# Attention and a gated feed-forward layer on one core: five PSUM banks for the last blocks of a stage, two for its outputs, and the outputs two blocks later

## The chip, the cores and the metric

The kernel runs on one core of a Trainium2 chip. The metric is the device time of one execution in microseconds; lower is better. A core has several engines, each with its own instruction queue, which it works through in order: TensorE (PE in the profile; its weight loads are PEld) multiplies matrices and writes to PSUM; VectorE (DVE) and ScalarE (ACT) work element by element and read PSUM and SBUF; GpSimd (POOL) does hardly anything here; SyncE (SP) starts DMA transfers. They meet at semaphores. PSUM has eight banks; a bank holds 512 fp32 numbers for each of 128 partitions.

## The reference

```python
def phi(x):
    proj = np.einsum('bhsd,df->bhsf', x, w_phi)
    proj = proj - np.max(np.abs(proj), axis=-1, keepdims=True)
    return np.concatenate([np.exp(proj), np.exp(-proj)], axis=-1)
q_p, k_p = (phi(q), phi(k))
kv = np.einsum('bhsf,bhsd->bhfd', k_p, v)
z = np.sum(k_p, axis=2)
num = np.einsum('bhsf,bhfd->bhsd', q_p, kv)
den = np.einsum('bhsf,bhf->bhs', q_p, z)[..., None] + 1e-06
x = (num / den) ... reshaped to (tokens, model width)
gate = 1.0 / (1.0 + np.exp(-(x @ w_gate)))
val = x @ w_val
out = (gate * val @ w_out)
```

There are 8 batches, 8 heads, 576 positions and a head width of 64; so 4608 tokens with a model width of 512. The feed-forward layer is 1536 wide. The change touches only the feed-forward part.

## The kernel before, in words

The feed-forward width is cut into 12 pieces of 128 columns, called j. **Stage one** works out the attention and, between its steps, the feed-forward part of the first four j (`JA = 4`) for all tokens. **Stage two** (`rest_chunks`, L293) adds the other eight j. Every fp32 number is split into a high and a low part (xh and xl, wh and wl, hh and hl), and three matmuls (high by high, high by low, low by high) stand for one.

*The feed-forward work of stage one* is built by `half_units` (L200). Tokens come in 18 chunks of 256, numbered 0 to 17. A chunk has four **blocks**, one for each j; a block has two halves, the gate columns (m = 0) and the value columns (m = 1), of 12 matmuls each (`half`, L239, with `mm_in`, L157 to L165). The first half takes a PSUM tile gv of one bank for both. When both halves are issued, the generator `gate` (L219) is started. It issues tanh t and exp u on ScalarE (L226, L227), which read the gate half; three steps on VectorE (L230, L231, L232), of which L231 is the last to read the bank; then hh on ScalarE (L234) and hl on VectorE (L236). Tiles hh and hl have ten buffers. A chunk also has two **outputs**, one for each 128 of its tokens (`half_out`, L253): 12 matmuls, three for each j (`mm_out`, L167 to L173), into a PSUM tile acc, then a copy y to SBUF on ScalarE (L261) and a store on SP one step later (L265). An output needs hh and hl of all four blocks of its chunk.

A chunk's input is loaded by `load_x` (L203): a DMA on SP (L206), three steps of waiting, then xh on ScalarE (L209), and one step later xl on VectorE (L211). It is begun when block 0 of the chunk ahead has been issued, if the attention has stored all of the chunk.

*Order.* Stage one runs under a schedule written by hand: each engine gets its instructions in the order in which the Python code issues them. Generators such as `gate`, `load_x` and the attention's own steps wait in a list `tasks`; `tick()` (L195) advances each by one `yield`. Closures for halves and outputs stand in a list `ready`. The attention's loop (L756 to L784) calls `fill()` (L681) between its steps, which pops as many closures as a budget (`RATE`, with a cost of 1.45 for a half and 0.69 times four for an output) allows, with a `tick()` behind each. Chunks wait in `coming` until the attention has got far enough. What is left when the attention is through, all of chunks 15 to 17 and the rest of 13 and 14 that stands in `ready`, is issued by L785 to L790, one closure and one `tick()` after the other. `chunk` (L272) sets the order in a chunk: block 0, first output of the chunk ahead, block 1, second output of the chunk ahead, block 2, block 3. The last chunk's outputs follow at the end.

*PSUM in stage one* (L358 to L360): two banks for gv (pool `ps_gv`), five for everything that the attention multiplies (pool `ps_a`, tag a), one for acc (pool `ps_o`). In a pool with n buffers a new tile takes the bank of the tile n before it, and the first matmul into it waits until that tile's readers are through.

*Stage two* has TensorE's order written by hand; its other engines are ordered by a scheduler that plans with a simulated timeline and places their instructions among those of stage one where it sees room. Each weight tile comes as raw 64-bit words (L106) and is converted on VectorE by six steps (L80, L82, L87, L90, L93, L94), with one on ScalarE (L81) and a DMA (L85). The weights of j = 4 to 7 go to memory that the attention has left, and so are converted while chunks 15 to 17 are on TensorE; those of j = 8 to 11 go to memory that stage one's weights and tiles hold to its end. Stage two's input is split by L62 and L63 (in `split`, L61). Its PSUM tiles are g and v, two banks each, and four banks for acc.

Of the kernel before, what the change touches and what calls it, by code (L numbers as in the profile page):

```python
# [9 lines left out]
F32 = mybir.dt.float32  # L10
# [11 lines left out]
P = 128  # L22
NP = H // 2
DM = H * D
# [4 lines left out]
CH = 256  # L29
# [5 lines left out]
JA = 4  # L35
# [9 lines left out]
def attention_moe(  # L45
# [106 lines left out]
    def x_tiles(mp, w, name):  # L152
        xh = mp.tile([P, NC4 * w], F32R, tag="xh", name="xh" + name)
        xl = mp.tile([P, NC4 * w], F32R, tag="xl", name="xl" + name)
        return xh, xl, xl.bitcast(F32)

    def mm_in(o, xs, j, m, w):  # L157
        (xh, xl), (wh, wl) = xs, weights[j]
        i = 0
        for cc in range(NC4):  # L160
            ws = slice(m * DM + cc * P, m * DM + cc * P + P)
            cs = slice(cc * w, cc * w + w)
            for a, x in ((wh, xh), (wh, xl), (wl, xh)):
                nc.tensor.matmul(o, a[:, ws], x[:, cs], start=i == 0, stop=i == 11)  # L164
                i += 1  # L165

    def mm_out(acc, t, hs, j, first, last):  # L167
        (hh, hl, _), (wh, wl) = hs, weights[j]
        ts, ws = slice(t * P, t * P + P), slice(2 * DM, 3 * DM)
        for i, (a, w) in enumerate(((hh, wh), (hh, wl), (hl, wh))):  # L170
            nc.tensor.matmul(  # L171
                acc, a[:, ts], w[:, ws], start=first and i == 0, stop=last and i == 2
            )  # L173
# [16 lines left out]
    def start(g):  # L190

        if next(g, tasks) is not tasks:
            tasks.append(g)

    def tick():  # L195
        for g in list(tasks):
            if next(g, tasks) is tasks:
                tasks.remove(g)

    def half_units(js, mp, ps_gv, ps_acc, need):  # L200
        xs, hs, gvs, parts = {}, {}, {}, collections.Counter()

        def load_x(c):  # L203
            xh, xl, raw = x_tiles(mp, CH, f"1_{c}")
            xs[c] = xh, xl
            nc.sync.dma_start(raw, xscr[c])  # L206
            for _ in range(3):
                yield
            act.copy(xh, raw)  # L209
            yield  # L210
            vec.tensor_tensor(xl, raw, xh.bitcast(F32), op=ALU.subtract)  # L211
            parts[c] = NP

        def begin(c):
            free = c < 2 or parts["v", c - 2] == len(js)
            if c not in xs and free and parts["x", c] == CH * NP:
                start(load_x(c))

        def gate(c, i, n):  # L219
            gv = gvs.pop((c, i))  # L220
            u = mp.tile([P, CH], F32, tag="u", name="u" + n)
            t = mp.tile([P, CH], F32, tag="t", name="t" + n)
            hh = mp.tile([P, CH], F32R, tag="hh", name="hh" + n, bufs=10)
            hl = mp.tile([P, CH], F32R, tag="hl", name="hl" + n, bufs=10)
            hs[c, i] = hh, hl, None
            act.activation(t, gv[:, 0, :], AF.Tanh, scale=0.5)  # L226
            act.activation(u, gv[:, 0, :], AF.Exp)  # L227
            yield
            tu = t.bitcast(U32)
            vec.tensor_scalar(tu, tu, 0x7FFFFFFF, None, op0=ALU.bitwise_and)  # L230
            vec.scalar_tensor_tensor(t, t, 1.0, gv[:, 1, :], op0=ALU.add, op1=ALU.mult)  # L231
            vec.scalar_tensor_tensor(u, u, 1.0, t, op0=ALU.min, op1=ALU.mult)  # L232
            yield
            act.copy(hh, u)  # L234
            yield
            vec.tensor_tensor(hl, u, hh.bitcast(F32), op=ALU.subtract)  # L236
            parts["h", c] += 1

        def half(c, i, m):  # L239
            while parts[c] < NP:  # L240
                begin(c)
                tick()
            need(js[i], m)
            n = f"1_{c}_{js[i]}"
            if m == 0:
                gvs[c, i] = ps_gv.tile([P, 2, CH], F32, tag="gv", name="gv" + n)
            mm_in(gvs[c, i][:, m, :], xs[c], js[i], m, CH)
            if m == 1:
                parts["v", c] += 1
                start(gate(c, i, n))  # L250
                begin(c + 1)

        def half_out(c, t):  # L253
            need(js[-1], 2)
            while parts["h", c] < len(js):
                tick()
            acc = ps_acc.tile([P, DM], F32, tag="acc", name=f"acc1_{c}_{t}")
            for i, j in enumerate(js):
                mm_out(acc, t, hs[c, i], j, i == 0, i == len(js) - 1)
            y = mp.tile([P, DM], F32, tag="y", name=f"y1_{c}_{t}")  # L260
            act.activation(y, acc, AF.Copy, scale=0.5)  # L261

            def store():
                yield
                nc.sync.dma_start(yscr[c][t], y)  # L265

            start(store())

        def unit(c, i):
            return [(1.45, lambda m=m: half(c, i, m)) for m in range(2)]  # L270

        def chunk(c):  # L272

            items = []
            for i in range(len(js)):
                items += unit(c, i)
                if i < 2:
                    items += outs(c - 1)[i : i + 1]
            return items

        def first():

            items = []
            for i in range(len(js)):
                items += unit(0, i) + unit(1, i)
            return items + outs(0)

        def outs(c):
            return [(0.69 * len(js), lambda t=t: half_out(c, t)) for t in range(2)]

        return chunk, first, outs, begin, xs, parts
# [60 lines left out]
    with ExitStack() as actx:  # L352
        actx.enter_context(tc.manual_schedule())
        wp1 = actx.enter_context(tc.tile_pool(name="wp1", bufs=1))
        moe = actx.enter_context(tc.tile_pool(name="moe1", bufs=2))
        at1 = actx.enter_context(tc.tile_pool(name="at1", bufs=1, side="right"))
        at = actx.enter_context(tc.tile_pool(name="at", bufs=2, side="right"))
        ps_gv = actx.enter_context(tc.tile_pool(name="ps_gv", bufs=2, space=PSUM))  # L358
        ps_a = actx.enter_context(tc.tile_pool(name="ps_a", bufs=5, space=PSUM))
        ps_acc = actx.enter_context(tc.tile_pool(name="ps_o", bufs=1, space=PSUM))  # L360
# [290 lines left out]
                t += w  # L651

        weighed = []

        def need(j, m):

            while len(weighed) <= 3 * j + m:
                grant(3 * j + m + 1)
                tick()

        chunk, first, outs, begin, xs, parts = half_units(list(range(JA)), moe, ps_gv, ps_acc, need)
        ready, coming = [], []
        cdone = wdone = spot = after = 0
        wq = []
# [16 lines left out]
        def fill(n=TICKS):  # L681
            nonlocal due, spot, after
            spot += 1
            if coming and coming[0][0] <= spot + AHEAD and coming[0][1]:
                begin(coming[0][2][0])
            while coming and coming[0][0] <= spot:
                b, cs = coming.pop(0)[1:]
                after = spot + 4 * NP + (0 if b else 6 + LAG[1] - LAG[0])
                if b == 0:
                    ready.extend(first())  # L690
                else:
                    for c in cs:
                        ready.extend(chunk(c))
            left = (coming[0][0] if coming else after) - spot
            due += min(RATE, sum(c for c, _ in ready) / max(1, left))
            while ready and due >= ready[0][0] / 2:
                cost, f = ready.pop(0)
                f()
                tick()
                due -= cost  # L700
                n -= 1
            for _ in range(n):
                tick()
# [52 lines left out]
        for i in range(EARLY - 1, N + 1):  # L756
            if EARLY <= i:
                load(i + 2)
                grant(3 * (i - 1))
            if i + 1 < N:  # L760
                keys(i + 1)
                copies(q_half(i + 1, 0))
                fill()
                copies(q_half(i + 1, 1))
                rest(i + 1)
                start(q_max(i + 1))
                fill()
            if i < EARLY:
                fill()
                fill()  # L770
                continue
            if i < N:
                kv(i)
            if i > EARLY:
                num(i - 1)
                if i % NP == 0:
                    queue(i // NP - 1)
            fill()
            if i < N:
                turn(i)  # L780
                start(q_exp(i))
                if i + 2 < N:
                    load_v(i + 2)
            fill()  # L784
        for _, _, cs in coming:  # L785
            for c in cs:
                ready.extend(chunk(c))
        for _, f in ready + outs(NCHUNK - 1):
            f()
            tick()  # L790
# [75 lines left out]
```

## Time and profile before

| | |
|---|---|
| median of three runs | 1295.95 us (1295.61 to 1300.03) |
| the profiled execution | 1297.41 us |
| its span (first to last instruction) | 1295.6 us |
| granted TensorE clock, mean | 0.97 |
| busy: TensorE, weight loads | 1228.6 us (95%), 970.1 us (75%) |
| busy: VectorE, ScalarE | 797.9 us (62%), 526.8 us (41%) |

A row of the timeline begins with the start in microseconds from the span's start and the duration; then come engine, line, operation, the tile written and the tiles read. Brackets hold the idle time of the engine just before, and behind the arrow what ended it. In a list of waits, "PE gv L164 <- DVE t L231" says that a matmul of L164 into gv waited for the VectorE instruction of L231. Tile names leave out buffer numbers, so all blocks look alike; which block a row belongs to follows from TensorE's written order, with 24 matmuls a block and 12 an output.

### The profile page before, as it was taken

To read this page: it belongs to the slowest core of one execution; us is meant where nothing else is said; L and a number is where in the kernel's file an instruction comes from. 1 tells how busy PE (TensorE), PEld (TensorE's weight loads), DVE (VectorE), ACT (ScalarE), POOL (GpSimd) and SP (SyncE) were. 2 spreads that over 40 slices of the span, in tenths; PEclk is the share of its full clock that TensorE was granted. 3 is DMA by queue.
4 is the path that set the end of the run, shared out by engine and by line. 5 is a ranking of instruction groups with operands and counts; after the bars stand their busy time and mean duration, and the time that the engine had idled before them with its cause. 6 is when DMAs were issued, how large, how long until landed. Compare 5 with 4: busy or idle time off the path is not lost.

```text
span 1295.6 us, 22470 instructions
## 1 busy us (share of the span) xinstructions
PE 1228.6 (95%) x9120; PEld 970.1 (75%) x9120; DVE 797.9 (62%) x1608; ACT 526.8 (41%) x1081; POOL 0.7 (0%) x6
## 2 busy tenths in 40 slices
PE   7848899999999999999889999999999999999998
PEld 5535566777777777777778888888888888888886
DVE  6699888788878778883894953424343434333333
ACT  4535556665565566564443422222222222222221
POOL 0000000000000000000000000000000000000000
PEclk8967899999999999999899999999999999999999
DMA  4556344343343334332763620202011111111010
GB/s 175 178 178 243 105 124 136 98 137 97 124 127 111 110 104 126 105 109 72 264 209 133 209 98 1 83 15 71 28 58 40 57 42 46 52 39 60 5 61 33
DMA packets 80868, 131.55 MB, mean 102 GB/s; under 512 B 18300, under 2 KB 37884, under 8 KB 80764
## 3 DMA queue, kind: packets, MB, share of 16 engines
q1 hardware_dynamic: 80764, 130.11, 30.9%
q8 instruction: 72, 1.18, 0.4%
q14 instruction: 32, 0.26, 0.1%
HBM read 92.04 MB, written 28.45 MB: 93 GB/s over the span
## 4 chain that ended last, share of the span: by engine, by line
PE 81%; DVE 11%; ACT 3%; issue 2%; DMA 2%; SPq 0%; DVEq 0%; ACTq 0%
PE acc L171 21%; PE g L164 15%; PE v L164 15%; PE gv L164 12%; PE kvz L528 5%; PE nm L580 4%; PE pq L411 2%; PE dp L591 2%; PE pk L421 2%; ACT eq L564 1%; PE kvz L542 1%; DMA wraw<-w_moe 1%; PE pk L482 1%; DVE mb L513 1%; PE tp L554 1%
## 5 line engine op out<-in xcount | busy, mean ns | idle before, releaser
L164 PE MATMUL gv<-xh,wh 128*128 128x256 f32 x576 | 174.5, 303 | 17.0 <-ACT xh L62 11.9
L171 PE MATMUL acc<-wh,hh 128*128 128x512 f32 x432 | 172.4, 399 | 3.4 <-ACT hh L234 2.7
L164 PE MATMUL gv<-xl,wh 128*128 128x256 f32 x576 | 167.2, 290 | 2.8 <-DVE xl L211 2.8
L171 PE MATMUL acc<-wh,hl 128*128 128x512 f32 x432 | 169.2, 392 | 0.7 <-DVE hl L236 0.7
L171 PE MATMUL acc<-wl,hh 128*128 128x512 f32 x432 | 169.1, 392 | 0.0
L164 PE MATMUL gv<-xh,wl 128*128 128x256 f32 x576 | 166.5, 289 | 0.0
L164 PEld LDWEIGHTS gv<-xh,wh 128*128 128x128 f32 x576 | 114.1, 198 | 34.6 <-issue 14.9
L62 ACT CAST hh<-u 128x512 fp32r<-128x512 f32 x72 | 44.7, 621 | 229.4 <-DVE u L185 229.4
L183 DVE TENSOR_SCALAR t<-t 128x512 uint32<-128x512 uint32 x72 | 30.7, 426 | 167.2 <-ACT t L180 167.2
L164 PEld LDWEIGHTS gv<-xl,wh 128*128 128x128 f32 x576 | 114.1, 198 | 3.9 <-DVE xl L211 3.0
L180 ACT ACTIVATE t<-g 128x512 f32<-128x512 f32 x72 | 43.0, 598 | 179.5 <-PE g L164 179.3
L164 PEld LDWEIGHTS gv<-xh,wl 128*128 128x128 f32 x576 | 114.0, 198 | 0.0
L164 PE MATMUL g<-xh,wh 128*128 128x512 f32 x288 | 113.0, 392 | 0.0
L164 PE MATMUL v<-xh,wh 128*128 128x512 f32 x288 | 112.6, 391 | 0.0
L164 PE MATMUL g<-xh,wl 128*128 128x512 f32 x288 | 112.5, 391 | 0.0
L164 PE MATMUL g<-xl,wh 128*128 128x512 f32 x288 | 112.5, 391 | 0.0
L164 PE MATMUL v<-xl,wh 128*128 128x512 f32 x288 | 112.3, 390 | 0.0
L164 PE MATMUL v<-xh,wl 128*128 128x512 f32 x288 | 112.1, 389 | 0.0
L184 DVE SCALAR_TENSOR_TENSOR t<-t,v 128x512 f32<-128x512 f32 x72 | 49.4, 686 | 97.7 <-PE v L164 97.7
L171 PEld LDWEIGHTS acc<-wh,hh 128*128 128x128 f32 x432 | 81.1, 188 | 26.2 <-issue 4.8
L171 PEld LDWEIGHTS acc<-wh,hl 128*128 128x128 f32 x432 | 81.2, 188 | 20.2 <-DVE hl L236 1.7
L171 PEld LDWEIGHTS acc<-wl,hh 128*128 128x128 f32 x432 | 81.3, 188 | 15.8
(92 smaller groups left out, 2120.5 us busy)
## 6 DMA issues: line engine op xcount, KB each, us to landing
wraw<-w_moe SPq DMA_DIRECT2D x36, 512.0 KB, 4.6
xl<-xs SPq DMA_DIRECT2D x34, 512.0 KB, 3.9
k<-k SPq DMA_DIRECT2D x32, 320.0 KB, 3.7
v<-v SPq DMA_DIRECT2D x32, 320.0 KB, 2.9
q<-q SPq DMA_DIRECT2D x32, 288.0 KB, 4.1
wh<-wtop SPq DMA_DIRECT2D x36, 256.0 KB, 2.3
ys<-y SPq DMA_DIRECT2D x36, 256.0 KB, 2.0
yp<-ys SPq DMA_DIRECT2D x36, 256.0 KB
```

The costliest lines, as they stand in the source:

```text
L62: a = act.copy(h, x)
L164: nc.tensor.matmul(o, a[:, ws], x[:, cs], start=i == 0, stop=i == 11)
L171: nc.tensor.matmul(acc, a[:, ts], w[:, ws], start=first and i == 0, stop=last and i == 2)
L180: act.activation(t, g, AF.Tanh, scale=0.5)
L183: vec.tensor_scalar(tu, tu, 0x7FFFFFFF, None, op0=ALU.bitwise_and)
L184: vec.scalar_tensor_tensor(t, t, 1.0, vl, op0=ALU.add, op1=ALU.mult)
L411: nc.tensor.matmul(pps[hd], wk[head(hd), :], x[head(hd), cs], start=True, stop=True)
L421: nc.tensor.matmul(pps[hd][:, t, :], kx[head(hd), t * P : t * P + P], wk[head(hd), :], start=True, stop=True,)
L482: nc.tensor.matmul(pp[:, 0, :], kx[:, 4 * P :], wk, start=True, stop=True)
L528: nc.tensor.matmul(kvz[o : o + Q, : 2 * F], vx[:, 2 * t + hd, o % D : o % D + Q], (e0, e1)[hd][:, t, :] if t < 4 else e2[:, 0, :], start=t ...
L580: nc.tensor.matmul(nms[hf][o : o + Q, :], w[:, sg, o : o + Q], es[sg][:, o // D, cs], start=sg == 0, stop=sg == 1, tile_position=(0, o),)
L591: nc.tensor.matmul(dp[o : o + Q, :], w[:, 2, z : z + Q], es[sg][:, hd, hf * HS : hf * HS + HS], start=sg == 0, stop=sg == 1, tile_position ...
```

## The change

Two things change for the feed-forward closures that are issued behind the attention's loop. The pools from which gv and acc are taken become entries of a dictionary, which `half` and `half_out` look up when they run; behind the loop the entries are replaced: gv then comes from the attention's five banks, acc from the two that gv had. And for the chunks that still wait in `coming` there, `chunk(c, 2)` puts the outputs of the chunk ahead behind block 2 and block 3 instead of 0 and 1. Closures that stand in `ready` already keep their place.

```diff
-    def half_units(js, mp, ps_gv, ps_acc, need):
+    def half_units(js, mp, homes, need):
...
             if m == 0:
-                gvs[c, i] = ps_gv.tile([P, 2, CH], F32, tag="gv", name="gv" + n)
+                ps, tag = homes["gv"]
+                gvs[c, i] = ps.tile([P, 2, CH], F32, tag=tag, name="gv" + n)
...
-            acc = ps_acc.tile([P, DM], F32, tag="acc", name=f"acc1_{c}_{t}")
+            ps, tag = homes["acc"]
+            acc = ps.tile([P, DM], F32, tag=tag, name=f"acc1_{c}_{t}")
...
-        def chunk(c):
+        def chunk(c, at=0):
 
             items = []
             for i in range(len(js)):
                 items += unit(c, i)
-                if i < 2:
-                    items += outs(c - 1)[i : i + 1]
+                if 0 <= i - at < 2:
+                    items += outs(c - 1)[i - at : i - at + 1]
             return items
...
+        homes = {"gv": (ps_gv, "gv"), "acc": (ps_acc, "acc")}
...
-        chunk, first, outs, begin, xs, parts = half_units(list(range(JA)), moe, ps_gv, ps_acc, need)
+        chunk, first, outs, begin, xs, parts = half_units(list(range(JA)), moe, homes, need)
...
+
+        homes.update(gv=(ps_a, "a"), acc=(ps_gv, "gv"))
         for _, _, cs in coming:
             for c in cs:
-                ready.extend(chunk(c))
+                ready.extend(chunk(c, 2))
         for _, f in ready + outs(NCHUNK - 1):
             f()
             tick()
```

## The prediction

> **What bounds the kernel now.** I read the page first, then TensorE's waits, then the stretch in which the change acts, engine by engine.
>
> ```profile
> span 1295.6 us, 22470 instructions
> PE 81%; DVE 11%; ACT 3%; issue 2%; DMA 2%; SPq 0%; DVEq 0%; ACTq 0%
> ```
>
> TensorE carries 81% of the chain that ended last, so time is won where TensorE waits or runs at a low clock. The stretches below (window, PE, PEld, DVE, ACT and POOL busy, granted clock, DMA share, GB/s) surround the change. In block names, 15.2 is block 2 of chunk 15, and o15.0 is that chunk's first output (12 matmuls).
>
> ```profile
> 624.10:635.12 11.02, 5.28 (x27) 4.88 (x27) 10.46 (x23) 5.54 (x8) 0.00 (x0) 0.69 0.87 318
> 635.12:649.22 14.10, 14.10 (x98) 13.09 (x96) 14.10 (x30) 6.63 (x14) 0.00 (x0) 1.00 0.61 205
> 680.29:691.66 11.37, 11.37 (x85) 10.88 (x84) 4.46 (x12) 3.62 (x9) 0.00 (x0) 1.00 0.12 46
> 635.12:698.58 63.46, 57.19 (x363) 50.70 (x362) 49.65 (x114) 24.91 (x55) 0.00 (x0) 0.97 0.48 158
> 698.58:760.00 61.42, 61.42 (x270) 50.50 (x269) 48.88 (x94) 22.16 (x35) 0.00 (x0) 1.00 0.50 167
> ```
>
> Until 635.12 TensorE stands for chunk 15's input; block 15.0 comes before any moved output, so this stays. From 635.12 to 698.58 come eleven blocks (15.1 to 17.3) and eight outputs (o14.0 to o17.1): this is the stretch that changes. From 698.58, where the second stage begins, TensorE is busy throughout, so what the stretch loses in length the kernel should lose. VectorE is full at first (14.10 of 14.10: it also converts the second stage's weights) and mostly idle from 680 on (4.46 of 11.37).
>
> TensorE's waits from 635 to 698.7 are these four groups (total, times, longest), 6.3 us together:
>
> ```profile
> PE acc L171 <- ACT hh L234: 2.7, 3, 1.4
> PE gv L164 <- DVE t L231: 2.2, 2, 1.5
> PE acc L171 <- ACT y L261: 0.7, 1, 0.7
> PE acc L171 <- DVE hl L236: 0.7, 2, 0.4
> ```
>
> TensorE in order of time (start, duration, the idle time before it and its releaser in brackets):
>
> ```profile
> 599.96 1.41 PE L591 MATMUL dp<-eq,kv 128*32 128x288 f32 x16
> 627.21 0.38 PE L164 MATMUL gv<-xh,wh 128*128 128x256 f32 x1 [2.90 <-ACT xh L209]
> 635.12 0.40 PE L171 MATMUL acc<-wh,hh 128*128 128x512 f32 x1
> 640.72 0.40 PE L171 MATMUL acc<-wh,hh 128*128 128x512 f32 x1
> 643.47 0.28 PE L164 MATMUL gv<-xh,wh 128*128 128x256 f32 x1
> 649.10 0.28 PE L164 MATMUL gv<-xh,wl 128*128 128x256 f32 x1
> 650.85 0.39 PE L164 MATMUL gv<-xh,wh 128*128 128x256 f32 x1 [1.47 <-DVE t L231]
> 657.46 0.50 PE L171 MATMUL acc<-wh,hh 128*128 128x512 f32 x1 [1.42 <-ACT hh L234]
> 658.63 0.80 PE L171 MATMUL acc<-wh,hl 128*128 128x512 f32 x1 [0.44 <-DVE hl L236]
> 659.23 0.41 PE L164 MATMUL gv<-xh,wh 128*128 128x256 f32 x1
> 661.79 0.34 PE L164 MATMUL gv<-xh,wh 128*128 128x256 f32 x1
> 695.73 0.50 PE L171 MATMUL acc<-wh,hh 128*128 128x512 f32 x1 [0.69 <-ACT y L261]
> 698.58 0.39 PE L164 MATMUL g<-xh,wh 128*128 128x512 f32 x1
> ```
>
> Two undisturbed blocks hold 48 matmuls; the first to the last takes 649.10 - 643.47 = 5.63 us for 47 steps, so 0.12 us each and 2.87 a block. An undisturbed output takes 643.47 - 640.72 = 2.75. Eleven blocks and eight outputs are 31.6 + 22.0 = 53.6 us; the stretch takes 63.46. **9.9 us are lost here**, 0.76% of the span. The waits are 6.3 of it. The rest is mostly matmuls spaced wide after a wait: from 659.23 to 661.79 twelve steps take 2.56 us where 1.44 would do.
>
> A sentence on that from the Trainium skill, "TensorE: Matmul & The Clock Gate", section "HAM oscillation — how this bites in real kernels": the clock is lost to idle gaps above about 3.4 us. The waits ahead of 659.23 are far shorter and the spacing doubled all the same, so by the page those 1.1 us would not go with the waits, and the ceiling would be 8.8 instead of 9.9.
>
> **The change part by part.**
>
> *Five banks for the blocks.* Nothing is added: the same matmuls write, the same gate reads. A block now waits for the gate five blocks back, not two. The attention's last matmuls start at 599.96, and its last bank is copied out by 601.49 + 0.40 (row below), and the pool hands out its oldest bank first; so that costs nothing. It removes the t L231 waits, 2.2 us and what follows them.
>
> *Two banks for the outputs.* Removes the y L261 wait, 0.7 us. The bank that an output takes was read by a gate two or more blocks earlier, so no wait is added.
>
> *Outputs behind blocks 2 and 3.* An output needs the hl of the preceding chunk's block 3. Before, one block and nine of its own matmuls stood between them; now three blocks do. For the last chunk, o16.1 stands between 17.3 and o17.0. This removes the hh L234 and hl L236 waits, 3.4 us. Each moved step also issues a copy y on ScalarE and a store on SP. On ScalarE y now stands ahead of hh of blocks 2 and 3 instead of 0 and 1; it waits for TensorE only, which will be ahead, so 0. On SP the store passes weight loads; nobody needs it before the second stage. o16.1, o17.0 and o17.1 follow each other and y has two buffers:
>
> ```profile
> ys<-y SPq DMA_DIRECT2D x36, 256.0 KB, 2.0
> ```
>
> o17.1's copy comes 5.5 us after o16.1's, the store between lands in about 2.0: nothing. Eight of ten hh/hl buffers are live at most: nothing.
>
> *What is late next: the gates.* Blocks and outputs without waits would end, counted on from 635.12: 15.3 at 646.5, 16.1 at 655.0, o15.1 at 666.2, 16.3 at 663.5, 17.2 at 674.8, o16.0 at 677.6, 17.3 at 680.5, o16.1 at 683.2, o17.1 at 688.7. The gates run on ScalarE and VectorE in a written order: tanh t and u, three VectorE steps, hh, then the next gate's t. So they have a pace of their own (first the attention's last copy out of a bank, then t and hh of a gate beside a mostly idle VectorE; then the t of 15.1, 15.2, 15.3, 16.0, 16.1 and, further on, 16.3):
>
> ```profile
> 601.49 0.40 ACT L607 COPY dr<-dp 128x288 f32<-128x288 f32 x1 [0.83 <-PE dp L591]
> 604.48 0.38 ACT L226 ACTIVATE t<-gv 128x256 f32<-128x256 f32 x1 [2.59 <-PE gv L164]
> 606.24 0.41 ACT L234 CAST hh<-u 128x256 fp32r<-128x256 f32 x1 [1.10 <-DVE u L232]
> ...
> 641.65 0.37 ACT L226 ACTIVATE t<-gv 128x256 f32<-128x256 f32 x1
> 647.46 0.38 ACT L226 ACTIVATE t<-gv 128x256 f32<-128x256 f32 x1
> 652.08 0.38 ACT L226 ACTIVATE t<-gv 128x256 f32<-128x256 f32 x1
> 657.32 0.38 ACT L226 ACTIVATE t<-gv 128x256 f32<-128x256 f32 x1
> 663.48 0.38 ACT L226 ACTIVATE t<-gv 128x256 f32<-128x256 f32 x1 [1.10 <-PE gv L164]
> 673.89 0.38 ACT L226 ACTIVATE t<-gv 128x256 f32<-128x256 f32 x1
> ```
>
> Beside the conversions a gate that waits for no block takes 4.6 (647.46 to 652.08) to 5.2 us (652.08 to 657.32), middle 4.9, and 5.8 with a chunk's xl in it (641.65 to 647.46); without them 606.24 + 0.41 - 604.48 = 2.2. TensorE would ask for one in 17.0 / 4 = 4.25 us. So the gates fall behind while conversions last, until about 680. Their t: 15.1 at 641.7 as now, 15.2 at 647.5, 15.3 at 652.1, 16.0 at 657.3, 16.1 at 662.2, 16.2 at 668.0, 16.3 at 672.9, 17.0 at 677.8, then 680.0, 682.2, 684.4. VectorE's rows for what hangs on them (hl of the undisturbed gate; a conversion step; xl of chunk 17; u of 16.1; hl of 16.3):
>
> ```profile
> 606.67 0.42 DVE L236 TENSOR_TENSOR hl<-u,hh 128x256 fp32r<-128x256 f32 x1
> 658.70 0.69 DVE L90 SCALAR_TENSOR_TENSOR wraw<-wraw 128x512 uint32<-128x512 uint32 x1
> 663.11 1.23 DVE L211 TENSOR_TENSOR xl<-xl,xh 128x1024 fp32r<-128x1024 f32 x1
> 666.99 0.42 DVE L232 SCALAR_TENSOR_TENSOR u<-u,t 128x256 f32<-128x256 f32 x1
> 679.48 0.42 DVE L236 TENSOR_TENSOR hl<-u,hh 128x256 fp32r<-128x256 f32 x1
> ```
>
> - Banks: the tightest is 17.3, whose turn comes at 677.6 and needs 16.2's t L231, which precedes its u, 3.5 us behind its t (666.99 - 663.48), so done by 671.5. Covered by 6.
> - Outputs: o16.0's tenth matmul is due at 677.6 - 0.7 = 676.9 and needs hl of 16.3, now at 679.48 + 0.42 = 679.9, 6.0 behind its t at 673.89, and then at 672.9 + 6.0 = 678.9: late by 2.0. o17.0's is due at 685.3; hl of 17.3 ends at 684.4 + 606.67 + 0.42 - 604.48 = 687.0: late by 1.7.
> - Input: the loader counts scheduler steps, and with the output gone from between blocks 0 and 1 xl of chunk 17 moves on VectorE from ahead of 16.1's gate to behind its u. That u ends at 662.2 + (666.99 + 0.42 - 663.48) = 666.1; with a conversion step of 0.69 and its own 1.23 it ends near 668, and 17.0 wants it at 666.3: late by 1.7.
>
> These three are the same lateness: a wait at 17.0 shifts the later dues too. So about 2.0 us once, plus 0.5 for wide spacing behind it. The stretch would end at 688.7 + 2.5 = 691.2. **Gain 9.9 - 2.5 = 7.4 us.** Bounds: gates that keep up leave 9.9; gates at 5.8 throughout put 16.1's t at 664.9, 17.0's xl near 670.7, 4.4 late, with spacing about 5.4, leaving 4.5. I take the middle pace because it comes from the two rows in which no block was awaited.
>
> The second stage's weights for j from 8 on are converted behind the release of the old ones by the last output, so that work shifts along with TensorE; it ran beside a TensorE without idle time (61.42 of 61.42): 0.
>
> The profiled execution took 1297.41 us, 1.8 outside its span; less 7.4 it is 1290.0. The three runs' median, 1295.95, lies 1.5 lower. From it: **1288.6 us**. About 0.5%, 6.5 us, is what a measurement of this kernel tells from no change; the line is at 1289.5.
>
> **The rivals.**
>
> 1. *The waits come back as waits for gates.* The written ScalarE and VectorE orders, not banks, are the limit, and conversions fill them. For it: VectorE's 14.10 of 14.10. Against it: its idle time after 680, into which gates can drain. At the pace of 5.8 the gain is 4.5, 1291.5; if the weight work is also re-ordered unfavourably by a single step per gate (0.69, for seven gates, 4.8), it is nothing, 1296. The Trainium skill speaks for this side in the same page and section: adding PSUM double-buffering to its thin-M kernel gave no further gain. Here t L231 stands among the releasers, so the trace agrees only in part.
> 2. *The gates pile up and the tail pays, slower.* With five banks TensorE can be five blocks ahead at 17.3 (680.5); o17.0 must then wait for all five. At 4.9 each they take 24.5 us, less 4.8 covered by o16.1 and nine matmuls: 19.7 lost, 9.8 more than gained, 1305.8. It turns slower by over 0.5% when five gates take 21.2, above 4.2 each. That needs conversions among them after 680, but all VectorE work of the stretch is 49.65 us, which would be done by 684.8.
> 3. *It doesn't do what it says.* If most blocks left were handed out before the banks are switched, little changes: 1296. Block 15.0 starts at 627.21, 26 us behind the attention's last group at 599.96 + 1.41, so I give it almost nothing.
>
> **How the numbers follow.** Forecast (gain 6.5 to 9.9): 0.56. Rival 1: 0.34, all within 0.5%. Rival 2: 0.06. Rival 3: 0.04, no change. Faster 0.56, same 0.38, slower 0.06. The range runs from the full 9.9 and 0.6 of spread between runs, 1285.5, to a gain of 2, 1294.0, which leaves out rival 2, rival 3 and the worst of rival 1.
>
> **What the changed profile would show.** Right: no waits on t L231 and y L261; the sum of waits between the stretch's ends about 2 us, on xl L211, hh L234 or hl L236 around 17.0, o16.0 or o17.0; the second stage's first g near 691; granted clock 0.99 there. If the first g stands at 695 or later, with hh or xl as releasers, rival 1; if one long wait stands ahead of o17.0, rival 2. If TensorE waits after the first g, the statement on the weights is wrong; if block 15.0 starts elsewhere than at 627, the order ahead of it was re-drawn, which I held fixed.

## The result, and the profile after

The changed kernel took 1289.43 us (median of six, 1286.48 to 1292.08), the kernel before 1297.98 us in the six runs that go with it. The ratio is 0.9931, interval 0.9914 to 0.9948: about 0.7% faster, where 7.4 us or 0.57% had been forecast. The profiled execution took 1289.85 us. From the page after, the span and the chain that ended last, which still runs over TensorE:

```profile
span 1288.1 us, 22464 instructions
...
PE 81%; DVE 10%; ACT 3%; DMA 3%; issue 2%; SPq 0%; DVEq 0%; ACTq 0%
```

The stretches of the kernel after, with the columns as before (window and its length, busy time of PE, PEld, DVE, ACT, POOL, clock, DMA share, GB/s):

```profile
625.43:636.48 11.05, 5.36 (x28) 4.96 (x27) 10.49 (x23) 5.54 (x8) 0.00 (x0) 0.69 0.88 323
636.48:690.86 54.38, 53.65 (x361) 49.35 (x360) 49.03 (x114) 24.07 (x55) 0.00 (x0) 1.00 0.55 184
690.86:752.00 61.14, 61.14 (x269) 50.28 (x268) 48.33 (x93) 21.77 (x35) 0.00 (x0) 1.00 0.51 168
```

VectorE does the same work as before, 49.03 against 49.65 us, in a shorter time, and TensorE's clock is 1.00 instead of 0.97. The second stage has no idle time again. TensorE's waits from 598 to 760:

```profile
PE gv L164 <- ACT xh L209: 2.8, 1, 2.8
PE gv L164 <- DVE xl L211: 2.8, 1, 2.8
PE acc L171 <- ACT hh L234: 0.7, 1, 0.7
PE nm L582 <- ACT eq L566: 0.4, 1, 0.4
```

The first two are chunk 15's input, as before. Of the 6.3 us in the stretch one wait of 0.7 is left. TensorE in order of time:

```profile
628.56 0.39 PE L164 MATMUL gv<-xh,wh 128*128 128x256 f32 x1 [2.85 <-ACT xh L209]
636.47 0.28 PE L164 MATMUL gv<-xh,wh 128*128 128x256 f32 x1
667.72 0.28 PE L164 MATMUL gv<-xl,wh 128*128 128x256 f32 x1
678.30 0.39 PE L171 MATMUL acc<-wh,hh 128*128 128x512 f32 x1
687.54 0.50 PE L171 MATMUL acc<-wh,hh 128*128 128x512 f32 x1 [0.73 <-ACT hh L234]
691.09 0.39 PE L164 MATMUL g<-xh,wh 128*128 128x512 f32 x1
```

Block 15.1 begins at 636.47 and the first g at 691.09. Call the time from the matmul behind block 15.0 to the first g the **stretch**: 54.62 us after, 63.46 before, 53.6 without any wait. It gave 8.84 us. The span fell by 1295.6 - 1288.1 = 7.5 only, because this execution came to 15.0 at 628.56 and the one before at 627.21, 1.35 later. That was lost ahead of everything that the change touches: up to the first moved output the rows of TensorE, VectorE and ScalarE come in the same order in both kernels. What follows the first g is 597.0 us in both.

A stretch differs between executions too. The changed kernel once more had 56.36, the kernel before once more 63.74, so the gain is 7.1 to 9.1 us. The start of 15.0 differs as well: the changed kernel once more came to it at 626.59, the kernel before once more at 628.21.

### The profile page after: what moved, and what is told of

Its sections match the earlier page's. It is cut to its first block, busy times and chain, and to the rows that moved or that the text cites. A ratio compares the mean times of both kernels' runs of the same rounds, so it can differ in the third digit from the quotient of the medians.

```text
span 1288.1 us, 22464 instructions
## 1 busy us (share of the span) xinstructions
PE 1221.7 (95%) x9120; PEld 964.7 (75%) x9120; DVE 798.1 (62%) x1608; ACT 525.4 (41%) x1081; POOL 0.7 (0%) x6
## 4 chain that ended last, share of the span: by engine, by line
PE 81%; DVE 10%; ACT 3%; DMA 3%; issue 2%; SPq 0%; DVEq 0%; ACTq 0%
PE acc L171 21%; PE g L164 15%; PE v L164 15%; PE gv L164 11%; PE kvz L530 5%; PE nm L582 4%; PE pq L413 2%; PE dp L593 2%; PE pk L423 2%; ACT eq L566 1%; PE kvz L544 1%; DMA wraw<-w_moe 1%; PE pk L484 1%; DMA rb<-den 1%; DVE t L231 1%
```

## The experiments

All stretches, in us, beside 53.6 without waits. Two numbers in a row are two executions; every other row is one.

| banks | order of outputs | conversions | stretch |
|---|---|---|---|
| as before | as before | as before | 63.46, 63.74 |
| new | as before | as before | 61.95 |
| as before | new | as before | 62.49 |
| five for blocks, one for outputs | new | as before | 59.58 |
| new | new | as before | 54.62, 56.36 |
| new | new, chunk 17's input later | as before | 60.30 |
| as before | as before | half the VectorE work | 59.30 |
| new | new | half the VectorE work | 53.56 |
| as before | as before | behind the last gate | 55.57, counted as said below |
| as before | as before | split | 62.79 |
| new | new | j = 4 held back | 62.80 |
| new | new | split | 53.63 |

**Banks alone.**

```diff
-                ready.extend(chunk(c, 2))
+                ready.extend(chunk(c))
```

> The changed kernel with its banks, but with the outputs behind blocks 0 and 1 as before. The stretch is counted from the matmul behind block 15.0 to the second stage's first g: 63.5 us before, 54.6 with the whole change, 53.6 without any wait. Theory (the gates' pace on ScalarE and VectorE sets when hh of a chunk's block 3 is there, and the bank waits are only spent ahead of the same lateness): the waits on t L231 vanish, those on hh L234 at o15.0 and o16.0 grow by as much; only the wait on y L261 is truly saved. Stretch 62 to 62.6, gain about 1 us. Rival (each wait is a loss by itself): the t L231 waits go with what follows them, stretch 59.8, gain 3.7 us.

Measured: 1296.32 us, ratio 0.999 (0.9978 to 1.0003), stretch 61.95. All waits in the stretch:

```profile
PE acc L171 <- ACT hh L234: 4.9, 3, 4.0
PE acc L171 <- DVE hl L236: 0.7, 2, 0.4
```

The waits on t L231 and y L261 are gone, and hh L234 grew from 2.7 to 4.9: at o15.0 it is 4.0 where it was 1.4. The bank wait had only been spent ahead of the same late gate. The theory holds.

**Order alone.**

```diff
-        homes.update(gv=(ps_a, "a"), acc=(ps_gv, "gv"))
```

> The changed kernel with its order of outputs, but with two banks for blocks and one for outputs as before. Theory (gates have a pace of about 4.7 us while VectorE converts): no wait on hh or hl at o15.0 and o16.0, but with two banks TensorE is held to the gates' pace at the three blocks that now follow each other without an output between: several waits on t L231, together 3 to 5 us; the y L261 wait stays. Stretch 58 to 59.5, gain 4 to 5.5 us. Banks and order together gave 8.8, so the sum of the two alone is less than both. Rival (each wait is a loss by itself): t L231 stays at 2.2 us in two waits, stretch 57.2, and both gains alone add up to the whole.

Measured: 1298.73 us, ratio 1.0002 (0.999 to 1.0015), stretch 62.49. The profiled execution came to 15.0 some 7 us late, so only its stretch is compared. In it:

```profile
PE gv L164 <- DVE t L231: 5.4, 4, 1.7
...
PE acc L171 <- ACT y L263: 1.6, 3, 0.7
```

The kind of wait is the one expected, its size was not: the stretch is 3 us longer than the range. The waits of 5.4 and 1.6 us, and 1.9 that goes with them (62.49 - 53.6 - 7.0), eat all but 1 us of the gain. It was not the clock, which stood at 1.00 in this stretch:

```profile
642.33:704.82 62.49, 55.47 (x363) 49.73 (x361) 49.30 (x114) 24.15 (x55) 0.00 (x0) 1.00 0.49 161
```

The banks alone give 1.5 and the order alone 1.0; both give 7.1 to 9.1. They are not two savings but one: each lets TensorE run ahead of late gates only if the other does too.

**One bank for the outputs.**

```diff
-        homes.update(gv=(ps_a, "a"), acc=(ps_gv, "gv"))
+        homes.update(gv=(ps_a, "a"))
```

> The changed kernel with five banks for blocks and the new order, but one bank for the outputs. Theory: only the three outputs that follow each other at the end (o16.1, o17.0, o17.1) and those behind gates that are late pay: y L261 waits of 0.7 at o17.0 and o17.1 and their doubled spacing, stretch 56 to 57.5, some 1.5 us behind the changed kernel. Rival (the second output bank is idle ornament): stretch 54.6 to 55.2.

Measured in one execution: stretch 59.58, 3 to 5 us behind the whole change, and both expectations were too low. TensorE's waits, and ScalarE beside the largest:

```profile
PE acc L171 <- ACT y L263: 4.8, 4, 2.5
```

```profile
667.90 0.50 PE L171 MATMUL acc<-wh,hh 128*128 128x512 f32 x1 [2.53 <-ACT y L263]
```

```profile
666.40 0.40 ACT L234 CAST hh<-u 128x256 fp32r<-128x256 f32 x1 [1.68 <-DVE u L232]
666.71 0.38 ACT L226 ACTIVATE t<-gv 128x256 f32<-128x256 f32 x1
666.99 0.38 ACT L227 ACTIVATE u<-gv 128x256 f32<-128x256 f32 x1
667.25 0.60 ACT L263 ACTIVATE y<-acc 128x512 f32<-128x512 f32 x1
```

The copy y that empties the only bank stands on ScalarE behind hh, t and u of late gates, and hh waits for VectorE. So the output bank comes free at the gates' pace as well. The second output bank covers that.

**Chunk 17's input two steps later.**

```diff
-            for _ in range(3):
+            for _ in range(5 if c == NCHUNK - 1 else 3):
                 yield
             act.copy(xh, raw)
```

> The changed kernel, with the input of chunk 17 copied two scheduler steps later, so that its xl stands on VectorE behind u of gate 16.2 instead of 16.1. In the changed kernel's profile this xl ended at 667.35, and its first reader in block 17.0 began at 667.72: 0.4 us to spare. Theory (the input's place on VectorE is at its edge): xl ends about one gate, 4.7 us, later; TensorE waits some 4.3 us for xl L211 at 17.0; later waits on hh disappear in it; first g 3.5 to 5 us later behind block 15.0 than in the changed kernel, stretch 58 to 59.5. Rival (there is room): no wait at 17.0 above 1 us, stretch 54.6 to 55.5.

Measured in one execution: stretch 60.30. VectorE and then TensorE:

```profile
669.64 1.21 DVE L211 TENSOR_TENSOR xl<-xl,xh 128x1024 fp32r<-128x1024 f32 x1
```

```profile
670.91 0.58 PE L164 MATMUL gv<-xl,wh 128*128 128x256 f32 x1 [3.77 <-DVE xl L211]
```

The wait is 3.8 us where 4.3 was expected, and the later waits on hh are gone. The stretch is 5.7 longer than 54.62 (3.9 longer than 56.36), 0.8 above the range: block 17.0 lost 2.6 more by matmuls that were spaced wide behind the wait. The input's place is at its edge.

**The changed kernel again.**

> The changed kernel itself, as the measure for the others on this chip: stretch 54.6 us, first g at 689.7 to 691.1, ratio to before 0.993.

Measured: 1288.73 us, ratio 0.9931 (0.991 to 0.9951). The ratio and the first g, at 690.51, are as expected; the stretch is 56.36, longer than expected, with these waits in it:

```profile
666.09 0.39 PE L164 MATMUL gv<-xl,wh 128*128 128x256 f32 x1 [0.54 <-DVE xl L211]
677.66 0.50 PE L171 MATMUL acc<-wh,hl 128*128 128x512 f32 x1 [0.27 <-DVE hl L236]
686.97 0.50 PE L171 MATMUL acc<-wh,hh 128*128 128x512 f32 x1 [0.83 <-ACT hh L234]
```

They stand at 17.0, o16.0 and o17.0. The first two are waits that the first execution had just escaped. So the change leaves the late gates at the edge, and small differences between executions decide what remains.

**Half the conversions,** with the old and the new banks and order. Three of VectorE's six steps for a weight tile are left out, among them those that put the low half of a number together. The edit, the same in both:

```diff
-        rest, unit = hi, lo
-        vec.tensor_scalar(hi, hi, 16, 0x01FF0000, ...)
-        vec.scalar_tensor_tensor(hi, lo, 16, hi, ...)
-        vec.tensor_scalar(unit, top, 0xFF800000, ...)
+        rest, unit = hi, top
```

> The kernel before without three of the six VectorE steps that convert a second-stage weight tile (the low halves of those weights are not the right ones; the count and shape of everything else stays): 1.8 us of VectorE a tile instead of 3.4. Theory (the waits come from gates that share VectorE with the conversions): the gates take some 3 us each in place of 4.9, and most of the waits go although banks and order are those of before: stretch 55 to 57.5 against 63.5. Rival (two banks and the early outputs are too few whatever VectorE does): stretch above 60.

> The changed kernel without the same three VectorE steps (the low halves of the second stage's weights are not the right ones). Theory: nothing is left to save but the wait ahead of the last outputs, stretch 53.6 to 54.3, so that beside half the conversions the change would be worth only 1.5 to 3.5 us. Rival: the same gain of about 8 us between this and the kernel before with half the conversions.

Measured in one execution each: 59.30 and 53.56, old form first:

```profile
633.33:692.63 59.30, 56.22 (x363) 50.88 (x361) 38.19 (x82) 25.61 (x56) 0.00 (x0) 0.97 0.53 175
632.98:686.54 53.56, 53.56 (x363) 49.68 (x361) 36.72 (x82) 25.34 (x56) 0.00 (x0) 1.00 0.58 192
```

The second stretch is as expected. The first lies between its theory and its rival, and so does the difference of the two, 5.7 us where 1.5 to 3.5 or about 8 was expected. With half of VectorE's conversions the old form still loses 5.7 us, the new form nothing. This pair alone does not settle how much of the loss the conversions cause.

**No conversions before the last gate,** old banks and order. A mark is kept of the last hl, and the VectorE and ScalarE steps of the weights j = 4 to 7 may only be issued behind it:

```diff
-            vec.tensor_tensor(hl, u, hh.bitcast(F32), op=ALU.subtract)
+            held["hl"] = vec.tensor_tensor(hl, u, hh.bitcast(F32), op=ALU.subtract)
...
-        return load, *from_f64(wh[:, ms], wl[:, ms], raw, sp, nb, f"{j}_{m}")
+        with ExitStack() as stack:
+            late = {j: "hl" for j in range(JA, JR)}
+            behind(stack, [held[late[j]]] if j in late else ())
+            done = from_f64(wh[:, ms], wl[:, ms], raw, sp, nb, f"{j}_{m}")
+        return load, *done
```

> The kernel before with every conversion of the weights for j = 4 to 7 held back until the last gate's hl is written, so that VectorE has only gates and inputs in the stretch. The stretch alone counts here: the second stage must then wait for its first weights, which makes the whole longer. Theory (the gates are late because conversions stand among them): with half the conversions 4.1 us of waits were left of 6.3 in the stretch (59.3 against 63.5); without any the gates take 2.2 to 2.9 us, the waits on t L231 and on hl or hh at o15.0 and o16.0 all go, and only y L261 and hh L234 at the last outputs stay, 0.7 and 0.2 us: stretch 54.3 to 55.3. Rival (two banks and the early outputs cost time whatever VectorE does): stretch above 57.

Measured in one execution: the last output's last matmul began at 689.51, and the first g at 693.59 after a wait of 3.68 for xh of the second stage's input. That wait is not counted: up to 689.67, behind the start of the last matmul, the stretch is 55.57, 0.3 above the range expected. (The 4.1 us of waits that the expectation gives for half the conversions hold 1.0 at 15.0; in the stretch it was 3.1.) The stretch, and TensorE's waits from 630 to 690, of which the first lies at 15.0:

```profile
634.10:689.67 55.57, 54.31 (x361) 49.50 (x360) 25.19 (x59) 19.41 (x47) 0.00 (x0) 1.00 0.14 50
```

```profile
PE acc L175 <- ACT y L265: 1.1, 1, 1.1
PE gv L168 <- DVE xl L215: 0.9, 1, 0.9
PE acc L175 <- ACT hh L238: 0.2, 1, 0.2
```

With VectorE at 25.19 of 55.57 us nothing waits from 15.1 to 17.3, with two banks and early outputs; only the last two outputs do. That settles it: the waits in the middle, with what goes with them 8 us of the 9.9, come from the conversions among the gates. What a conversion takes on ScalarE and in DMA is held back here too (DMA share 0.14 against 0.48), so this run alone does not single out VectorE; the one before, which left out VectorE steps only, won 4.2 us. The banks and the order do not make the gates earlier; they let TensorE do without them for longer.

**Conversions of j = 4 held back,** in the changed kernel, behind xl of chunk 15 (the same edit with `late = {JA: NCHUNK - 3}` and a mark of that xl in `load_x`).

> The changed kernel, with the conversion of the second stage's first three weight tiles (j = 4) held back until xl of chunk 15 has been written. In the changed kernel TensorE waits 5.7 us for this input at block 15.0, while hh of 14.2, t of 14.3 and then xh and xl stand behind gates that share VectorE with these conversions. Theory (it is the conversions that delay the input, not its DMA): xh and xl come about 4 us earlier, the waits at 15.0 shrink from 5.7 to 1 to 2 us, and 15.0 runs at full clock, 1.3 us more. The conversions then last some 6 us longer and the last gates are later by 2 to 3. Net 2 to 4 us faster than the changed kernel. Rival (the input's DMA and the attention's last steps set the time): the waits at 15.0 stay above 5 us, and the later conversions make it slower by 1 to 3 us.

Measured: 1295.06 us, ratio 0.997 (0.996 to 0.9981), slower than the changed kernel, where 2 to 4 us faster was expected. The waits at 15.0 fell from 5.7 to 2.8 us, not to the 1 to 2 of the theory, and the stretch is 62.80. The outputs at its end and the last 15 us:

```profile
682.17 0.50 PE L174 MATMUL acc<-wh,hh 128*128 128x512 f32 x1 [1.02 <-ACT y L266]
685.74 0.50 PE L174 MATMUL acc<-wh,hh 128*128 128x512 f32 x1 [1.92 <-ACT hh L237]
689.15 0.80 PE L174 MATMUL acc<-wh,hh 128*128 128x512 f32 x1 [2.08 <-ACT hh L237]
```

```profile
680.00:695.29 15.29, 10.18 (x31) 6.98 (x29) 9.09 (x23) 5.29 (x12) 0.00 (x0) 0.78 0.44 150
```

Conversions now ran among the last gates, and the tail paid. The theory had the direction at the input right and priced this loss at 2 to 3 us; it was 6 to 8. The prediction's second rival, gates that pile up ahead of the last outputs, is real: it only needs VectorE work in that place.

**Conversions split:** j = 4 behind xl of chunk 15, j = 7 behind the last gate (`late = {JA: NCHUNK - 3, JR - 1: "hl"}`).

> The changed kernel with the conversions of j = 4 held back until xl of chunk 15 is written, and those of j = 7 held back until the last gate's hl is written. Holding j = 4 alone brought the input 2.9 us earlier, but the conversions then ran among the last gates, and the outputs at the end waited 5 us at a lowered clock. Theory (VectorE's work before the last gate is the limit): with 10 us of conversions moved behind the last gate the gates keep up again; waits at 15.0 of 3 us as with j = 4 alone, stretch 54 to 55.5; 3 to 4.5 us faster than the changed kernel, about 0.990 of before, if j = 7 to 11 are still converted before TensorE needs them. Rival (the second stage's first weights come late): waits of TensorE on wl or wh behind the first g, and no gain over the changed kernel.

Measured: 1286.03 us, ratio 0.9897 (0.988 to 0.9913). This has the lowest median, 2.7 us under the changed kernel in its second comparison, but the two intervals (there 0.991 to 0.9951) just touch, so the step from one to the other is not clear of noise by the times alone. The waits at 15.0 are 3.0 us, as expected, and the stretch is below its range of 54 to 55.5. The stretch and what follows:

```profile
634.12:687.75 53.63, 53.63 (x362) 49.75 (x362) 45.77 (x105) 24.81 (x55) 0.00 (x0) 1.00 0.51 169
687.75:760.00 72.25, 72.25 (x318) 59.38 (x317) 63.86 (x122) 27.95 (x42) 0.00 (x0) 1.00 0.58 190
```

TensorE has no idle time in either, so the weights of j = 7 to 11 are still in time and the rival is out.

**The same split with the old banks and order.**

> The kernel before with the conversions split as in the fastest version (j = 4 behind xl of chunk 15, j = 7 behind the last gate), but its own banks and order. Theory: j = 5 and 6 still stand among the gates for some 20 us of VectorE, so o15.0 or o16.0 still waits, but later gates are free: stretch 57 to 60, with the changed banks and order it was 53.6. Rival (the split alone does it): stretch below 55, and the banks and the order are not needed any more.

Measured in one execution: stretch 62.79, under 1 us better than 63.46 and 63.74, and outside the range expected. Without the change the split is worth next to nothing in the stretch; with the change it brings the stretch to its floor. Of 6.1 us of waits 4.7 lie between 647 and 662, where the conversions of j = 5 and 6 still stand among the gates, as the theory had it; their price was set too low.

**The kernel before, again.**

> The kernel before once more, for the spread of the stretch between executions: the changed kernel's was 54.6 in one and 56.4 in another. Theory (the waits before come from orders that are fixed in the program): 62.5 to 64.5, with the same releasers; what differs between executions lies ahead of 600 us, in the attention.

Measured: stretch 63.74 with the same four kinds of waits, 6.5 us in all. The first statement holds, the second in the main: of the 1.45 us by which the first g came later, 1.0 was there at the start of 15.0.

## Why the prediction was right

*The direction and the place.* The gain comes from the stretch alone, and no wait came up behind the first g. The floor of 53.6, worked out from two undisturbed rows, was the right one: with VectorE relieved two kernels reached it.

*The size.* Forecast: 9.9 less 2.5 that the late gates would leave. The two executions left 1.0 and 2.8. So the sum is right within their spread, and the lateness is where it was put: the three places named, 17.0, o16.0 and o17.0, are those at which the second execution waited. In the first, the pace reckoned was slightly too slow. In order, t of 15.2, 15.3, 16.0, 16.1 and 17.0 in the kernel after:

```profile
647.95 0.37 ACT L226 ACTIVATE t<-gv 128x256 f32<-128x256 f32 x1
653.42 0.38 ACT L226 ACTIVATE t<-gv 128x256 f32<-128x256 f32 x1
657.47 0.38 ACT L226 ACTIVATE t<-gv 128x256 f32<-128x256 f32 x1
661.82 0.38 ACT L226 ACTIVATE t<-gv 128x256 f32<-128x256 f32 x1
...
676.31 0.38 ACT L226 ACTIVATE t<-gv 128x256 f32<-128x256 f32 x1
```

The six gates from 15.2 to 17.0 took 676.31 - 647.95 = 28.36 us, 4.7 each with chunk 17's input among them; the forecast had 677.8 - 647.5 = 30.3, 5.05 each. So the two places that were to be late by 1.7 and 2.0 were just in time: VectorE's rows for xl of chunk 17 and hl of 16.3, and the twelfth matmul of o16.0, the first to read that hl,

```profile
666.13 1.22 DVE L211 TENSOR_TENSOR xl<-xl,xh 128x1024 fp32r<-128x1024 f32 x1
677.76 0.42 DVE L236 TENSOR_TENSOR hl<-u,hh 128x256 fp32r<-128x256 f32 x1
678.75 0.39 PE L171 MATMUL acc<-wh,hl 128*128 128x512 f32 x1
```

show that xl and hl end at 667.35 and 678.18, with 0.4 us to spare before its reader at 667.72 and 0.6 before that at 678.75. Only the third, hh of 17.3 ahead of the tenth matmul of o17.0, stayed late, by 0.7 where 1.7 was reckoned. The working let the tenth matmul of an output wait for hl. The tenth, at 678.30 in o16.0, reads hh; hl is read 0.45 later, so the lateness at both outputs was reckoned up to 0.45 too large.

*What was luck.* The time came out only 0.8 us off, 1288.6 against 1289.43, since two errors partly cancel: the median of three runs from which it was counted lies 2.0 below the 1297.98 of six, and the gain forecast lies 1.2 below the 8.55 between the medians. The first g, forecast at 691.2, came at 691.09 because 15.0 began 1.35 later and the stretch was 1.5 shorter than reckoned. A start of 15.0 elsewhere than at 627 was named as the sign of an order drawn anew. It began at 628.56, the order ahead of it is the same, and the kernel before itself came once at 628.21; the sign was too strict.

*What was mis-sized: the parts.* The prediction gave the order 3.4 us of waits, the five banks 2.2 and the two output banks 0.7, as if each would go with its own edit. The order alone gave 1.0, all banks alone 1.5, and the second output bank 3 to 5 on top of the rest. That last term was mis-sized most. It was read off the one wait on y in the profile before, and the working said of the moved y that "it waits for TensorE only". In the changed kernel, where no wait on y is left, that cost nothing. But y stands on ScalarE behind gates that wait for VectorE, so with one bank it holds TensorE up. The total came out since it was reckoned as the ceiling less the lateness of the gates, with all three edits made together.

*The rivals.* The first was wrong about the whole change and right about its parts: either alone leaves waits for late gates, and the lateness comes from where it said. The second did not happen here, and did when conversions were put among the last gates. The third did not happen.

*The clock.* The prediction put the ceiling at 9.9 and took the wide spacing for a part of the waits. The two kernels at 53.6 reached 9.9, so it was.

## What to carry to other kernels

When several engines' waits alternate ahead of one late chain, price them together: removing one wait lets the next come due, and only when buffers and order both cover the lateness does the sum appear. Before adding buffers, ask how late the chain is and why; here a background job on VectorE, placed by a scheduler among due work, was the cause, and splitting it around the critical places took the stretch to its floor once the buffers were there. A copy that frees a buffer is as late as the queue in which it stands.

## What the runs showed of the hardware

Short waits cost more than their length. With j = 4 held back, TensorE waited 5.0 us in the stretch, no wait above 2.08, and the stretch was 62.80 - 53.6 = 9.2 us too long; the granted clock was 0.78 over its last 15.29 us, in which all the waits lie. "TensorE: Matmul & The Clock Gate" of the Trainium skill, section "HAM oscillation — how this bites in real kernels", names gaps above about 3.4 us as the ones to avoid. The wait of 3.77 us at 17.0, with chunk 17's input two steps later, agrees: the clock was 0.94 over that stretch. But with j = 4 held back three gaps of 1 to 2 us within 9 us were enough, and the measurement decides for this kernel.

Length alone does not decide. A wait of 2.53 us by itself, with one bank for the outputs, and waits of 1.75 and 1.14 us whose ends lie 4.3 us apart, with the order alone, left the clock at 1.00 over their stretches. No run here varied only the distance between gaps, so the rule behind this stays open.
